# A second v buffer, a single g buffer, ungated output weights and an earlier first weight load in a fused attention and MLP kernel

## The chip, the cores and the metric

The kernel runs on one core of one Trainium2 chip. The metric is the device time of one execution in microseconds (us), lower is better. Before the change the median was 353.1 us (three executions, 352.37 to 354.01). Every number below comes from a timed run or from the trace of a profiled run on the chip. The profiled span is about 2 us shorter than the time of the same execution, so spans are compared with spans and times with times.

## The reference

Causal attention with a forget gate over 8 batches x 8 heads x 576 tokens x 64, and then a two-layer MLP with exact gelu on its 4608 x 512 result:

```python
scores = scale * np.matmul(q, k.transpose(0, 1, 3, 2))
cum = np.cumsum(np.log(np.clip(f, 0.0001, 1.0)), axis=-1)
scores = np.where(causal, -1e9, scores + cum[..., :, None] - cum[..., None, :])
attn = softmax(scores)                       # over the last axis
x = np.matmul(attn, v)                       # heads side by side: 4608 x 512
h = x @ w_in                                 # 512 x 2048
out = gelu(h) @ w_out                        # 2048 x 512
```

## The kernel before

TensorE (PE in the profile) does everything large: scores, attention times v, gemm1 (x times w_in), gemm2 (gelu result times w_out). gemm2 of a batch is spread as filling between the attention steps of the next batch, and then gemm1 of that next batch runs in one stretch, with ScalarE (ACT) taking the gelu of each 128 x 512 result into one of 16 g tiles. GpSimd (POOL) multiplies v by the decay weights ("weighing") and also issues the loads of q, k and of the weights; SyncE (SP) issues the loads of v and the transposing DMAs.

The parts that the change and the argument touch:

```python
g_pool = ctx.enter_context(tc.tile_pool(name="g", bufs=2))   # 16 tags g0..g15
m_psum = ctx.enter_context(tc.tile_pool(name="m_psum", bufs=2, space=PSUM))
...
v_sb = consts.tile([P, H, NBLK, D], FP32)          # one v buffer
nc.gpsimd.memset(v_sb[:, :, 0, 0:1], 0.0)          # gates the load behind it
load_v(0, 0, 4)                                    # SP's queue
load_qk_tokens(0, 6, 8)                            # GpSimd's queue
load_v(0, 4, 8)
...
# in first_attention (batch 0)
weigh_v(0, 0)
load_w_in(0)
load_w_in(1)
weigh_v(0, 1)
load_qk_tokens(1, 0, 4)
weigh_v(0, 2)
weigh_v(0, 3)
load_w_in(2)
load_w_in(3)
nc.gpsimd.memset(v_sb[:, :, 0, 0:1], 0.0)          # v of batch 1 waits for this
load_v(1, 0, 4)
load_v(1, 4, 8)
load_qk_tokens(1, 4, 8)
...
def x_tail_dma(b):                                 # last 64 tokens of a batch
    nc.sync.dma_start_transpose(
        tails[:, :, b * TL : (b + 1) * TL],
        xt_of[b][D:P].rearrange("p i h d -> p (i h d)"))
...
def gemm1(c, ffb):
    ...                                            # 4 matmuls into a m_psum tile
    nc.scalar.activation(g_of[c][ffb], ps, Act.Gelu)
...
# in the loop over batches, behind the attention of batch 0
if b == 0:
    load_w_out(0)
    x_tail_dma(0)
for ffb in range(n_ff):
    gemm1(b, ffb)
    ...
        if ffb == 9:
            weigh_v(1, 0)
            for c in range(1, 4):
                load_w_out(c)
```

The softmax here doesn't subtract the row's maximum and nothing guards it: scores larger than these inputs give would overflow.

## Time and profile before

| | before |
|---|---|
| time, median of three | 353.1 us |
| profiled span | 350.2 us |
| PE busy | 338.7 us (97%) |
| start of gemm1 of batch 0 | 27.83 us |
| first matmul with w_out | 44.72 us |
| start of gemm1 of batch 1 | 70.90 us |
| batch period in the steady part | 36.57 us |

PE is the bound, and only time in which PE stands still, or is made to, moves the result.

From the page of the kernel before, two groups of instructions (line, engine, operation, out<-in, count, busy time, mean of one in ns, idle time just before them and what ended it), and one group of DMA issues, whose last column is the median time from issue to landing in us:

```profile
L392 PE MATMUL ps<-xT,w_in_sb 128*128 128x512 bf16 x512 | 112.6, 379 | 0.7 <-ACT xT L371 0.6
L430 PE MATMUL ps<-w_out_sb,g 128*128 128x512 bf16 (+2 forms) x208 | 44.3, 363 | 0.0
w_out_sb<-in_moe_w_out_dram POOLq DMA_DIRECT2D x4, 512.0 KB, 9.3
```

Neither gemm waits: 0.7 us of idle time before all gemm1 matmuls, 0.0 before gemm2 of the first and the last batch, which are the ones on this line. The weights of gemm2 land 9.3 us after their issue, as the median of four; the first quarter takes 15.6.

### The profile page before, as it was taken

Reading aid. Unit: us, or ns where it says so; the run is one execution under the profiler, and the core shown is the slowest. Engines: PE = TensorE matmul, PEld = TensorE weight load, DVE = VectorE, ACT = ScalarE, POOL = GpSimd, SP = SyncE. Lnnn points to the kernel's source line nnn. Section 1 sums busy time; section 2 is a strip of 40 time slices with the busy share of each in tenths; the row PEclk is TensorE's granted clock in tenths of the full one; section 3 lists DMA queues with packets and bytes.
Section 4 is the critical chain, followed back from the end, with each engine's and each line's share of the span. In section 5 each row is a group of like instructions: output and inputs, shape, how many; then the busy total and the mean of one; then the engine's idle time right before and its main releaser. Section 6 shows DMA issues by size and latency. Waiting matters only on the chain.

```text
span 350.2 us, 7729 instructions
## 1 busy us (share of the span) xinstructions
PE 338.7 (97%) x3082; PEld 174.8 (50%) x3082; DVE 203.0 (58%) x499; ACT 216.1 (62%) x298; POOL 124.5 (36%) x243
## 2 busy tenths in 40 slices
PE   8998989999999999999999999999999999999995
PEld 3564534544555455545554455445544554444443
DVE  4561984496469935894579557956696563011011
ACT  5877585457874687468746874687567774603600
POOL 8291185415538044613453245514350530000000
PEclk9999999999999999999999999999999999999999
DMA  7999989974994998298928794679510131011013
GB/s 108 181 176 196 199 143 195 214 175 95 206 163 136 136 206 156 85 135 137 220 76 128 143 196 99 104 135 213 126 37 2 47 85 45 0 62 60 0 32 90
DMA packets 101219, 43.24 MB, mean 123 GB/s; under 512 B 80000, under 2 KB 96640, under 8 KB 101184
## 3 DMA queue, kind: packets, MB, share of 16 engines
q1 hardware_dynamic: 83888, 28.60, 40.1%
q0 software_dynamic: 16896, 13.63, 26.0%
q8 instruction: 24, 0.39, 0.5%
q10 hardware_dynamic: 400, 0.52, 0.4%
q14 instruction: 11, 0.09, 0.1%
HBM read 36.85 MB, written 9.44 MB: 132 GB/s over the span
## 4 chain that ended last, share of the span: by engine, by line
PE 83%; ACT 9%; POOL 2%; issue 2%; DMA 2%; SPq 1%; DVE 0%; ACTq 0%; POOLq 0%
PE ps L392 36%; PE ps L479 18%; PE ps L430 12%; PE o L332 9%; PE s L296 7%; ACT e L311 5%; ACT L311 2%; DMA v_sb<-in_v_dram 2%; ACT g L404 1%; POOL vw L279 1%; PE ps_x L368 1%; SPq L114 1%; POOL k L102 1%; POOL q L102 0%; PE s L305 0%
## 5 line engine op out<-in xcount | busy, mean ns | idle before, releaser
L404 ACT ACTIVATE g<-ps 128x512 bf16<-128x512 f32 x144 | 86.0, 597 | 82.2 <-PE ps L392 82.2
L311 ACT ACTIVATE e<-s 128x896 bf16<-128x896 f32 (+1 forms) x128 | 103.9, 862 | 30.7 <-PE s L296 25.5
L392 PE MATMUL ps<-xT,w_in_sb 128*128 128x512 bf16 x512 | 112.6, 379 | 0.7 <-ACT xT L371 0.6
L479 PE MATMUL ps<-w_out_sb,g 64*128 64x512 bf16 (+1 forms) x690 | 102.4, 376 | 0.0
L313 POOL TENSOR_SCALAR_AFFINE_SELECT e<-e 128x256 bf16<-128x256 bf16 x135 | 53.4, 406 | 113.5 <-ACT e L311 112.5
L392 PEld LDWEIGHTS <-w_in_sb 128*128 128x128 bf16 x576 | 56.0, 98 | 68.1 <-issue 2.9
L279 POOL TENSOR_TENSOR vw<-v_sb,wT 128x640 bf16<-128x640 f32 x32 | 41.0, 1280 | 47.5 <-DMA v_sb<-in_v_dram 15.8
L296 PE MATMUL s<-qT,kT 64*128 64x320 bf16 (+4 forms) x384 | 47.9, 282 | 4.0 <-ACT e L311 3.4
L479 PEld LDWEIGHTS <-g 64*128 64x128 bf16 (+1 forms) x690 | 37.7, 94 | 25.4 <-issue 1.6
L263 DVE COPY qT<-tq 64x288 bf16<-64x288 bf16 x96 | 45.1, 470 | 1.5
L332 PEld LDWEIGHTS <-e 128*128 128x128 bf16 x960 | 35.9, 98 | 17.6 <-issue 11.5
L430 PE MATMUL ps<-w_out_sb,g 128*128 128x512 bf16 (+2 forms) x208 | 44.3, 363 | 0.0
L332 PE MATMUL o<-vw,e 128*128 128x65 bf16 x960 | 41.7, 194 | 0.8 <-ACT e L311 0.4
L487 DVE COPY ot<-ps 128x512 f32<-128x512 f32 x24 | 16.5, 689 | 36.0 <-PE ps L479 36.0
L439 DVE COPY ot<-ps 128x512 f32<-128x512 f32 (+2 forms) x13 | 8.4, 650 | 48.9 <-PE ps L430 48.7
L296 PEld LDWEIGHTS <-kT 64*128 64x128 bf16 x384 | 20.1, 94 | 28.7 <-issue 15.6
L263 DVE COPY kT<-tk 64x288 bf16<-64x288 bf16 x96 | 32.3, 336 | 1.6
L347 DVE RECIPROCAL r<-o 128x5 f32<-128x5 f32 x64 | 12.5, 195 | 30.1 <-PE o L332 29.3
L348 DVE TENSOR_TENSOR x<-o,r 128x256 bf16<-128x256 f32 x64 | 27.2, 425 | 2.2
L430 PEld LDWEIGHTS <-g 128*128 128x128 bf16 x208 | 18.8, 98 | 18.9 <-issue 0.4
L358 DVE TENSOR_SCALAR xt<-o,r 64x64 bf16<-64x64 f32 x60 | 17.4, 290 | 1.4
L489 DVE TENSOR_TENSOR ot<-ot,ps 128x512 f32<-128x512 f32 x24 | 16.5, 687 | 1.3
(60 smaller groups left out, 144.7 us busy)
## 6 DMA issues: line engine op xcount, KB each, us to landing
out_dram<-ot SPq DMA_DIRECT2D x32, 256.0 KB, 2.4
v_sb<-in_v_dram SPq DMA_DIRECT2D x20, 256.0 KB, 4.6
v_sb<-in_v_dram SPq DMA_DIRECT2D x29, 128.0 KB, 5.5
q<-in_q_dram POOLq DMA_DIRECT2D x6, 576.0 KB, 6.5
k<-in_k_dram POOLq DMA_DIRECT2D x6, 576.0 KB, 8.6
w_in_sb<-in_moe_w_in_dram POOLq DMA_DIRECT2D x4, 512.0 KB, 7.9
w_out_sb<-in_moe_w_out_dram POOLq DMA_DIRECT2D x4, 512.0 KB, 9.3
q<-in_q_dram POOLq DMA_DIRECT2D x4, 144.0 KB, 4.4
```

What stands on the lines that cost most here:

```text
L263: nc.vector.tensor_copy(rows[:, odd], src[odd * D : (odd + 1) * D, 2 * i + h].rearrange("d j p -> d p j"),)
L279: nc.gpsimd.tensor_tensor(vw_of[b][:, hs, :, 0:D], v_sb[:, hs, :, :], w.unsqueeze(3).to_broadcast([P, 2, NBLK, D]), Alu.mult,)
L296: nc.tensor.matmul(st[:, h, c : c + w], kT[i][d, K0[n] : K0[n] + P], qT[i][d, q0 : q0 + w], start=True, stop=not on_pe or c not in SDIAG[t],)
L311: nc.scalar.activation(et[:, :, 0:c], st[:, :, 0:c], Act.Exp, scale=scale)
L313: nc.gpsimd.affine_select(out=et[:, :, c0 : c0 + P], in_=et[:, :, c0 : c0 + P], compare_op=Alu.is_ge, fill=0.0, base=0, pattern=[[0, 2], [ ...
L332: nc.tensor.matmul(o[:, m, :], e_of[b, i, t][:, h, c : c + P], vw_of[b][:, 2 * i + h, n, :], start=(n == 0), stop=(n == m),)
L348: nc.vector.tensor_tensor(x_of[b, i][:, :, h, :], o[:, 0:4, 0:D], r[:, 0:4].unsqueeze(2).to_broadcast([P, NBLK - 1, D]), Alu.mult,)
L358: nc.vector.tensor_scalar(*tail, r[D:P, 4:5], None, Alu.mult)
L392: nc.tensor.matmul(ps, w_in_sb[:, kt, ffb * P : (ffb + 1) * P], src[:, kt, :], start=(kt == 0), stop=(kt == n_dm - 1),)
L404: nc.scalar.activation(g_of[c][ffb], ps, Act.Gelu)
L430: nc.tensor.matmul(pss[ts][:, c0:c1], g_of[c][kt][:, ts * P : (ts + 1) * P], w_out_sb[:, kt, c0:c1], start=(kt == 0), stop=(kt == n_ff - 1),)
L479: nc.tensor.matmul(banks[r], g_of[c][kt][rows, ts * P : (ts + 1) * P], w_out_sb[rows, kt, :], start=(kt == 0), stop=last if r else kt == n ...
```

## The change

The intent: bring the loads of the first 50 us forward. v gets a second buffer, so v of batch 1 is queued right behind v of batch 0 instead of waiting until that one has been weighed. The four w_out quarters are queued without the former gates, behind w_in and q and k of batch 1. The first w_in quarter is issued ahead of the first weighing. And the g tiles go from two buffers to one.

```diff
-    g_pool = ctx.enter_context(tc.tile_pool(name="g", bufs=2))
+    g_pool = ctx.enter_context(tc.tile_pool(name="g", bufs=1))
...
-    v_sb = consts.tile([P, H, NBLK, D], FP32)
+    v_of = [consts.tile([P, H, NBLK, D], FP32, name=f"v_sb{i}") for i in range(2)]
...
     load_v(0, 4, 8)
+    load_v(1, 0, 4)
+    load_v(1, 4, 8)
...
+    nc.vector.memset(v_of[1][0:D, :, 4, :], 0.0)
...
+        gate = x_pool.tile([P, 1], FP32, tag="gate", name="gate")
+        nc.gpsimd.tensor_copy(gate, v_of[0][:, 0, 2, 0:1])
+        load_w_in(0)
         weigh_v(0, 0)
-        load_w_in(0)
         load_w_in(1)
...
-        nc.gpsimd.memset(v_sb[:, :, 0, 0:1], 0.0)
-        load_v(1, 0, 4)
-        load_v(1, 4, 8)
         load_qk_tokens(1, 4, 8)
+        for c in range(4):
+            load_w_out(c)
...
         if b == 0:
-            load_w_out(0)
             x_tail_dma(0)
...
                     weigh_v(1, 0)
-                    for c in range(1, 4):
-                        load_w_out(c)
+                    weigh_v(1, 1)
                     load_qk_tokens(2)
-                    weigh_v(1, 1)
```

More of the change, by code (lines that the diff above doesn't have):

```diff
@@ L114, in load_v @@
             nc.sync.dma_start(
-                v_sb[p0:P, h0:h1, n, :],
+                v_of[b % 2][p0:P, h0:h1, n, :],
                 v[b, h0:h1, K0[n] + p0 : K0[n] + P].rearrange("h p d -> p h d"),
@@ L136 @@
     )
-    nc.gpsimd.memset(v_sb[:, :, 0, 0:1], 0.0)
+    nc.gpsimd.memset(v_of[0][:, :, 0, 0:1], 0.0)
     load_v(0, 0, 4)
@@ L172 @@
     nc.scalar.activation(lf, f_sb, Act.Ln)
-    nc.vector.memset(v_sb[0:D, :, 4, :], 0.0)
+    nc.vector.memset(v_of[0][0:D, :, 4, :], 0.0)
     nc.vector.tensor_tensor_scan(cum, ones, lf, 0.0, Alu.mult, Alu.add)
     nc.scalar.activation(wk, cum, Act.Exp, bias=cum[:, S // 2 : S // 2 + 1], scale=-1.0)
+    nc.vector.memset(v_of[1][0:D, :, 4, :], 0.0)
     def warm_up(n):
@@ L280, in weigh_v @@
             vw_of[b][:, hs, :, 0:D],
-            v_sb[:, hs, :, :],
+            v_of[b % 2][:, hs, :, :],
             w.unsqueeze(3).to_broadcast([P, 2, NBLK, D]),
@@ L541, in first_attention @@
         load_w_in(3)
-        nc.gpsimd.memset(v_sb[:, :, 0, 0:1], 0.0)
-        load_v(1, 0, 4)
-        load_v(1, 4, 8)
         load_qk_tokens(1, 4, 8)
+        for c in range(4):
+            load_w_out(c)
         scores(0, 2, 0)
```

## The prediction

> **What bounds the kernel now.** I began with the page. TensorE (PE) is busy nearly all the time; ScalarE, VectorE and GpSimd are far from it.
>
> ```profile
> PE 338.7 (97%) x3082; PEld 174.8 (50%) x3082; DVE 203.0 (58%) x499; ACT 216.1 (62%) x298; POOL 124.5 (36%) x243
> ```
>
> So PE idles 350.2 - 338.7 = 11.5 us in all, and nothing can gain more than that. The windows view says where: a steady batch (144 to 181 us) has PE busy 36.70 of 37.00 us, the last 58 us idle 3.6 (mostly the closing stores), the first 70 us some 6. The change works on loads of the first 50 us, so I read that part instruction by instruction. In the timeline (start, duration, what, and the idle time before it with what ended it), only one PE gap there is ended by weighted v, which is what the change wants to bring forward:
>
> ```profile
> 15.00 1.28 POOL L279 TENSOR_TENSOR vw<-v_sb,wT 128x640 bf16<-128x640 f32 x1 [6.53 <-DMA v_sb<-in_v_dram]
> 16.36 1.58 POOL L155 DMA_DIRECT2D w_in_sb<-in_moe_w_in_dram  x2
> 17.95 1.30 POOL L279 TENSOR_TENSOR vw<-v_sb,wT 128x640 bf16<-128x640 f32 x1
> 19.46 0.64 PE L332 MATMUL o<-vw,e 128*128 128x65 bf16 x15 [0.28 <-POOL vw L285]
> ...
> 42.79 1.28 POOL L279 TENSOR_TENSOR vw<-v_sb,wT 128x640 bf16<-128x640 f32 x1 [15.65 <-PE ps L392]
> 44.16 2.31 POOL L159 DMA_DIRECT2D w_out_sb<-in_moe_w_out_dram  x3
> ```
>
> GpSimd waits 15.65 us for v of batch 1 (its fourth DMA of the first half was issued at 26.9 and took 15.3 us to land, 42.2), and w_out queues behind that. But in the view of waits PE never waits for w_out, w_in or batch 1's vw. These late loads are hidden.
>
> The diff has one more line: g goes from two buffers to one. So I read ScalarE around the switches between exp (L311) and gelu (L404):
>
> ```profile
> 63.81 0.70 ACT L311 ACTIVATE e<-s 128x640 bf16<-128x640 f32 x1 [0.36 <-PE s L296]
> 64.54 1.28 ACT L404 ACT_TABLE_LOAD   x1
> 71.96 0.60 ACT L404 ACTIVATE g<-ps 128x512 bf16<-128x512 f32 x1 [6.14 <-PE ps L392]
> ...
> 84.91 0.60 ACT L404 ACTIVATE g<-ps 128x512 bf16<-128x512 f32 x1 [0.27 <-PE ps L392]
> 85.52 1.28 ACT L311 ACT_TABLE_LOAD   x1
> ```
>
> The gelu table is loaded at 64.54, right after the last exp, 6 us before the first gemm1 matmul at 70.90. It costs nothing, in all seven later batches alike (the last is at 286.42, first gelu 291.67).
>
> **What the Trainium skill says.** "ScalarE: Activation LUTs", What ACT_TABLE_LOAD costs: a load takes about 1283 ns, plus a drain of about 1380. The trace agrees on the load (1.28 us) but shows no such drain: from load to first exp it is 86.82 - 85.52 = 1.30. "Perfetto Trace Analysis", Identifying Dependency Chains: an instruction that waits for several engines may get event-semaphore instructions put ahead of it. The trace has these, and what they cost is below. "DMA: Bandwidth & Descriptors", Queues, rings and completion order: each DMA engine takes turns between the queues that have work. So v of batch 1, behind v of batch 0 in the same queue, cannot delay it, but takes a share from the weights on GpSimd's queue. The before trace fits: v of batch 1 took up to 15.3 us to land beside the weights, v of batch 0 at most 6.1.
>
> **The change part by part.** I compared the instruction streams of the two builds, which gives order and waits, no times. PE's stream is the same row for row. Four things differ.
>
> 1. Weighing. One w_in issue (0.8 us) instead of two lies between the first two weighings, so the second comes 0.8 us earlier: the 0.28 gap at 19.46 closes. The first weighing keeps its 15.00: the gate waits for the third v DMA (issued 7.7, landed after 5.9, so 13.6), the w_in issue then ends near 14.5, and the fifth v DMA lands at 14.86. Gain 0.28 us.
>
> 2. VectorE clears the second v buffer (0.48 us, as L173) between the scan, which ends at 6.15, and the first kT copy, so that copy starts near 6.65 instead of 6.31 and ends at 7.41. The first scores start at 7.53, behind warm-up matmuls that end at 7.50. Loss at most 0.05 us.
>
> 3. v, w_out and q, k of batch 2 come earlier. PE waited for none of them: gain 0. Could v delay the weights? It is 8 x 576 x 64 x 4 = 1.18 MB. From 15 to 20 us the DMA moved 98 GB/s against some 200 when full, so about 5 x 102 KB = 0.5 MB fits in idle time; the other 0.7 MB pushes what is queued then by at most 3.4 us. Landing times before, plus 3.4, against first use: batch 1's first half of k 28.1, 31.5, used at 34.3; third w_in quarter 31.0, 34.4, used at 35.4. Nothing is late, though the last has only 1 us.
>
> 4. One g buffer. gemm2 of a batch has ended, in PE's order, before gemm1 of the next begins, so the data are free in time. But each gelu now also carries a wait on ScalarE's own semaphore, and with two waits the first is put on the instruction ahead. For the first gelu of batches 1 to 7 that is the table load: in the stream of after these seven loads wait for PE and the gelu behind waits only for ScalarE. Since that gelu needs its PSUM tile, the wait on the load must be the one for gemm1's first group. The load comes onto the path. This is my main term.
>
> Its size, from single records and semaphore updates of the trace (batch 1): first gemm1 matmul 70.896; the fourth's semaphore 71.934. A table load that waits for PE exists already at exp of batch 1: semaphore 44.381, load 44.448 (0.067 later), exp 45.742. So the first gelu starts at 71.934 + 0.067 + 1.294 = 73.295 instead of 71.957 and ends 0.597 later at 73.892. m_psum has two buffers, so gemm1's third group waits for this gelu; a stalled PE resumes 0.05 after it ends (batch 0: 0.04 to 0.05), 73.94, instead of 72.620. Stall 1.32 us, and PE is the bound, so it is all paid: 7 x 1.32 = 9.2 us.
>
> The second wait costs too. A gelu with one wait starts 0.023 us after PE's semaphore; an instruction with two has the event semaphore ahead and starts 0.083 after. In batch 1 PE's third group starts 0.057 after the semaphore of the gelu's end and needs about 0.042: slack 0.015, and 0.06 more makes a stall of 0.045 per pair of groups. The before kernel shows exactly this in its final gemm1, whose gelus have two waits already:
>
> ```profile
> 72.82 0.60 ACT L404 ACTIVATE g<-ps 128x512 bf16<-128x512 f32 x1 [0.27 <-PE ps L392]
> 74.55 0.60 ACT L404 ACTIVATE g<-ps 128x512 bf16<-128x512 f32 x1 [0.27 <-PE ps L392]
> ...
> 320.30 0.60 ACT L404 ACTIVATE g<-ps 128x512 bf16<-128x512 f32 x1 [0.34 <-PE ps L392]
> 322.07 0.60 ACT L404 ACTIVATE g<-ps 128x512 bf16<-128x512 f32 x1 [0.31 <-PE ps L392]
> ```
>
> 1.77 for two groups there, 1.73 in batch 1. After the table stall six pairs remain in a batch: 6 x 0.045 = 0.27, x 7 = 1.9 us. The final gemm1 pays already. The last gelu of a batch is 0.06 later, and the chain from it to the exp table and exp sets when PE goes on:
>
> ```profile
> 84.91 0.32 ACT g L404
> 85.22 0.30 issue
> 85.52 1.19 ACT L311
> 86.71 0.11 issue
> 86.82 0.93 ACT e L311
> 87.74 0.04 issue
> 87.78 0.37 PE s L296 x2
> ```
>
> For six of the seven batches an exp follows: 6 x 0.06 = 0.4 us.
>
> Sum: 9.2 + 1.9 + 0.4 - 0.28 + 0.05 = 11.3 us. 353.1 + 11.3 = 364.4 us.
>
> **The rivals.** (a) As intended: the loads come earlier and time falls. For it: GpSimd waits 15.8 us for v and 15.6 at L279. Against: GpSimd is 36% busy and PE's stream waits for it only 0.28. It would give 352 to 353. (b) The single buffer costs nothing, because the load's wait is met early (if it were gemm2's old reads, done at about 70.8, the load would end near 72.2, and only 0.2 us a batch be lost): 354 to 356. Against: the wait must cover the first group's tile. (c) The load is exposed but the two-wait term is absorbed: 353.1 + 9.0 = 362. Against: the final gemm1 shows it. (d) Weights collide with v and gemm1 of batch 0 stalls at its third quarter: 1 to 2 us on top, 366. For it: the margin of 1 us; against: before, v already competed with that very quarter.
>
> **Range and chances.** (c) and (d) bound the likely outcomes, with 0.8 us for the scatter of the before runs (352.37 to 354.01): 362.2 to 366.2. The line of 2% lies at 360.2, 4 us below my sum; to stay under it the table term would have to halve, and it rests on an exact wait and on a load length that every table load of the trace shows. Slower 0.93, within 2% 0.06, faster 0.01.
>
> **What would show it.** In the profile after: seven gelu table loads with an idle time before them ended by PE ps and the gelu 1.29 later; a PE gap of about 1.3 us in gemm1 before its third group, ended by ACT g; gelus spaced 1.77 per pair in batches 1 to 7; the batch period 36.6 going to about 38.2; no PE gap at the second weighed pair; GpSimd's 15.65 us wait gone without effect. I am wrong if the loads still run right after the last exp, or if PE's gap is elsewhere.

## More of the kernel before

From PE's timeline of the kernel before (start, duration, what, and in brackets the idle time before it with what ended it), the place where the first w_out quarter is needed:

```profile
44.60 0.29 PE L305 MATMUL s<-after,ident_bf 128*128 128x128 bf16 x2
44.72 1.03 PE L430 MATMUL ps<-w_out_sb,g 128*128 128x512 bf16 x4
```

The first w_out matmul follows without a gap at 44.72. By the trace's records this quarter had landed at 41.98, 2.7 us earlier.

## The result and the profile after

The changed kernel took 369.38 us (median of four executions: 367.37, 369.38, 369.38, 370.50), against 353.56 us of the kernel before on the same chip. The ratio is 1.043, with a 95% interval of 1.035 to 1.051: slower. Ratios here are the mean time of the fast executions of one kernel over the mean of those of the other from the same rounds, so they are not quite the ratio of the medians. The predicted 364.4 us had the direction right; the time lies 3 us above the predicted range (362.2 to 366.2).

The page of the changed kernel, in the lines that answer to those of before (its L396, L408 and L434 are L392, L404 and L430 of before):

```profile
PE 342.2 (94%) x3040; PEld 175.5 (48%) x3082; DVE 203.4 (56%) x500; ACT 215.5 (59%) x298; POOL 124.5 (34%) x243
...
L396 PE MATMUL ps<-xT,w_in_sb 128*128 128x512 bf16 x503 | 114.6, 378 | 9.5 <-ACT g L408 8.1
...
L434 PE MATMUL ps<-w_out_sb,g 128*128 128x512 bf16 (+2 forms) x200 | 44.0, 366 | 2.5 <-DMA w_out_sb<-in_moe_w_out_dram 1.9
...
L408 ACT ACT_TABLE_LOAD x8 | 10.3, 1283 | 39.6 <-PE ps L396 39.5
...
w_out_sb<-in_moe_w_out_dram POOLq DMA_DIRECT2D x4, 512.0 KB, 23.0
```

Three things are new. PE idles 365.3 - 342.2 = 23.1 us in place of 11.5. gemm1 waits 8.1 us for gelus, and the gelu table loads now wait for PE: that was predicted. And gemm2's first matmul waits 1.9 us for w_out, whose loads now take 23.0 us from issue to landing in place of 9.3 (medians of four; the first quarter 20.6 in place of 15.6): that was not.

**The predicted part.** ScalarE's timeline of the changed kernel around the switch to gelu in batch 2:

```profile
114.27 1.28 ACT L408 ACT_TABLE_LOAD   x1 [5.53 <-PE ps L396]
115.56 1.08 ACT L408 ACTIVATE g<-ps 128x512 bf16<-128x512 f32 x2
117.33 0.60 ACT L408 ACTIVATE g<-ps 128x512 bf16<-128x512 f32 x1 [0.68 <-PE ps L396]
118.19 0.60 ACT L408 ACTIVATE g<-ps 128x512 bf16<-128x512 f32 x1 [0.27 <-PE ps L396]
119.10 0.60 ACT L408 ACTIVATE g<-ps 128x512 bf16<-128x512 f32 x1 [0.31 <-PE ps L396]
```

The table load waits 5.53 us for PE's first gemm1 group; in the kernel before it ran directly behind the last exp. The gelu starts 1.29 us after it. From there the gelus come 1.77 us a pair (117.33 to 119.10) where before they came 1.73 a pair. PE's timeline, batch 1, shows what this does:

```profile
77.79 6.54 PE L396 MATMUL ps<-xT,w_in_sb 128*128 128x512 bf16 x28 [1.16 <-ACT g L408]
```

**The part that was not predicted.** PE's timeline of the changed kernel where w_out is first needed:

```profile
45.84 0.29 PE L309 MATMUL s<-after,ident_bf 128*128 128x128 bf16 x2
48.05 0.60 PE L434 MATMUL ps<-w_out_sb,g 128*128 128x512 bf16 x1 [1.92 <-DMA w_out_sb<-in_moe_w_out_dram]
...
51.50 1.03 PE L434 MATMUL ps<-w_out_sb,g 128*128 128x512 bf16 x4
```

PE waits 1.92 us, and the first matmul after the wait takes 0.60 us. The clock records say why: PE runs at half clock from 48.09 to 51.50 us. The Trainium skill, "TensorE: Matmul & The Clock Gate", What's actually happening, describes a free-running window of 3413 ns over which TensorE's activity is watched to set the clock; the records agree with the length, 3.413 us.

Why was w_out late? It was issued at 27.38 us, 1 us later than before (26.37), but landed at 48.00 in place of 41.98. The windows view of the changed kernel gives, for each stretch of time, the busy time of each engine with the number of instructions, then the granted clock, the DMA share and the DMA rate in GB/s:

```profile
38.00:41.70 3.70, 3.65 (x21) 1.71 (x20) 3.57 (x8) 2.12 (x4) 0.00 (x0) 1.00 1.25 195
41.70:46.10 4.40, 4.40 (x38) 2.13 (x36) 4.24 (x10) 2.80 (x5) 0.00 (x0) 1.00 1.63 38
46.10:50.00 3.90, 1.76 (x6) 0.53 (x6) 1.74 (x4) 2.60 (x3) 0.00 (x0) 0.75 1.25 203
```

For 4.4 us the DMA engines moved 38 GB/s, while their packets show as in flight all along (a share of 1.63, for packets of two queues at once); before and after that they moved 195 and 203. In the packet records, 26 packets of both queues stand for up to 4.3 us and are all released between 46.07 and 46.13 us, just as the last DMA of v of batch 1 lands (46.15). Directly behind that DMA in SP's queue stands the transposing DMA of the first x tail:

```profile
32.33 5.12 SPq L384 DMA_TRANSPOSE tails<-xt  x1
```

It was issued at 32.33 and landed at 47.93. In the kernel before, it was issued at 42.54, when GpSimd's queue was nearly empty, and landed 2.46 us later.

**The sum of the profiled runs.** The first and the last column of numbers are positions in PE's timeline, in us; the three between them are the lengths of the parts from one position to the next. The second trace of the changed kernel and the two mended kernels are explained under the experiments.

| kernel | gemm1 of batch 0 starts | from there to the first w_out matmul | from there to gemm1 of batch 1 | from there to PE's end | PE's end |
|---|---|---|---|---|---|
| before | 27.83 | 16.89 | 26.18 | 275.54 | 346.44 |
| changed | 29.07 | 18.98 | 26.70 | 286.83 | 361.58 |
| changed, second trace | 29.14 | 20.67 | 26.74 | 286.87 | 363.42 |
| changed, tail moved | 27.80 | 16.89 | 26.17 | 286.85 | 357.71 |
| changed, tail moved, table loaded early | 28.14 | 16.88 | 26.17 | 278.21 | 349.40 |

The first changed row against before: 1.24 + 2.09 + 0.52 + 11.29 = 15.14 us. The last term is the predicted one, 9.2 + 1.9 + 0.4 = 11.5. The second and third are the late w_out and the half clock after it. The first is a late start, in which PE happened to stay at half clock until 10.54 us (before: until 5.24).

### The profile page after: what moved, and what is told of

The parts are those of the page before. It is cut to its first block, busy times and chain, and to the rows that moved or that the text cites. A ratio compares the mean times of both kernels' runs of the same rounds, so it can differ in the third digit from the quotient of the medians.

```text
span 365.3 us, 7799 instructions
## 1 busy us (share of the span) xinstructions
PE 342.2 (94%) x3040; PEld 175.5 (48%) x3082; DVE 203.4 (56%) x500; ACT 215.5 (59%) x298; POOL 124.5 (34%) x243
## 4 chain that ended last, share of the span: by engine, by line
PE 72%; ACT 11%; DMA 6%; issue 4%; POOL 4%; SPq 2%; DVE 0%; ACTq 0%; POOLq 0%
PE ps L396 28%; PE ps L483 17%; PE ps L434 12%; PE o L336 8%; PE s L300 6%; DMA w_out_sb<-in_moe_w_out_dram 6%; ACT e L315 4%; ACT g L408 3%; SPq L114 2%; ACT L315 2%; ACT L408 2%; POOL vw L283 1%; POOL k L102 1%; POOL q L102 1%; PE ps_x L372 1%
## 5 line engine op out<-in xcount | busy, mean ns | idle before, releaser
L396 PE MATMUL ps<-xT,w_in_sb 128*128 128x512 bf16 x503 | 114.6, 378 | 9.5 <-ACT g L408 8.1
L408 ACT ACTIVATE g<-ps 128x512 bf16<-128x512 f32 x144 | 85.2, 597 | 54.9 <-PE ps L396 54.7
L483 PE MATMUL ps<-w_out_sb,g 64*128 64x512 bf16 (+1 forms) x666 | 96.2, 377 | 1.0
L396 PEld LDWEIGHTS <-w_in_sb 128*128 128x128 bf16 x576 | 55.5, 97 | 79.5 <-issue 19.6
L283 POOL TENSOR_TENSOR vw<-v_sb,wT 128x640 bf16<-128x640 f32 x32 | 40.9, 1277 | 27.4 <-PE o L336 11.0
L434 PE MATMUL ps<-w_out_sb,g 128*128 128x512 bf16 (+2 forms) x200 | 44.0, 366 | 2.5 <-DMA w_out_sb<-in_moe_w_out_dram 1.9
L267 DVE COPY qT<-tq 64x288 bf16<-64x288 bf16 x96 | 43.4, 452 | 1.5
L336 PEld LDWEIGHTS <-e 128*128 128x128 bf16 x960 | 35.8, 98 | 17.1 <-issue 10.9
L267 DVE COPY kT<-tk 64x288 bf16<-64x288 bf16 x96 | 34.1, 355 | 1.6
L434 PEld LDWEIGHTS <-g 128*128 128x128 bf16 x208 | 18.9, 98 | 21.4 <-DMA w_out_sb<-in_moe_w_out_dram 2.1
```

The costliest lines, as they stand in the source:

```text
L267: nc.vector.tensor_copy(rows[:, odd], src[odd * D : (odd + 1) * D, 2 * i + h].rearrange("d j p -> d p j"),)
L283: nc.gpsimd.tensor_tensor(vw_of[b][:, hs, :, 0:D], v_of[b % 2][:, hs, :, :], w.unsqueeze(3).to_broadcast([P, 2, NBLK, D]), Alu.mult,)
L336: nc.tensor.matmul(o[:, m, :], e_of[b, i, t][:, h, c : c + P], vw_of[b][:, 2 * i + h, n, :], start=(n == 0), stop=(n == m),)
L396: nc.tensor.matmul(ps, w_in_sb[:, kt, ffb * P : (ffb + 1) * P], src[:, kt, :], start=(kt == 0), stop=(kt == n_dm - 1),)
L434: nc.tensor.matmul(pss[ts][:, c0:c1], g_of[c][kt][:, ts * P : (ts + 1) * P], w_out_sb[:, kt, c0:c1], start=(kt == 0), stop=(kt == n_ff - 1),)
L483: nc.tensor.matmul(banks[r], g_of[c][kt][rows, ts * P : (ts + 1) * P], w_out_sb[rows, kt, :], start=(kt == 0), stop=last if r else kt == n ...
```

## The experiments

An execution is called slow here when it is more than 1.5% above the fastest of the same kernel. Where a kernel itself has two kinds of executions, this rule calls the longer kind slow, and the ratio of the fast runs leaves it out. Where that happens below, all times are listed.

### 1. One g buffer alone (g1_only)

```diff
 # the kernel before
-    g_pool = ctx.enter_context(tc.tile_pool(name="g", bufs=2))
+    g_pool = ctx.enter_context(tc.tile_pool(name="g", bufs=1))
```

> The kernel before with one edit: one g buffer instead of two. Theory (the table load and the second wait come onto the path): +11.3 us, 364 to 365 us, ratio about 1.032; seven gelu table loads that wait for gemm1's first group, a PE gap of about 1.2 us ended by ACT g in each of batches 1 to 7, gelus 1.77 us apart per pair, and no PE wait for w_out. Rival (the loads that come early did the harm, the single g buffer is cheap): 353 to 355 us.

Measured: 363.64 us (362.88 to 364.26) against 352.77, ratio 1.030 (1.028 to 1.033). PE waits 8.1 us in seven waits for the gelu, as in the changed kernel, and never for w_out. So the single g buffer alone costs 10.9 us, two thirds of the loss, and the rest belongs to the loads.

### 2. One g buffer, gelu table loaded early (g1_preload)

```diff
 # the kernel before with g bufs=1, and
+    tab = consts.tile([P, 2], FP32)
+    nc.vector.memset(tab, 0.0)
...
                 scores(b, i, t)
+                if (i, t) == (HP - 1, 3):
+                    nc.scalar.activation(tab[:, 1:2], tab[:, 0:1], Act.Gelu)
...              # and the same two lines in second_attention
```

A gelu of one column behind the last exp of batches 1 to 7 makes the table load run there, where ScalarE has nothing to wait for.

> The kernel before with one g buffer, and a gelu of a 128x1 tile behind the last exp of batches 1 to 7, so that the gelu table is loaded there, without a wait. Theory: the 7 x 1.32 = 9.2 us of the load go, the second wait (1.9 + 0.4 us) and the small gelus stay: 353.5 + 2.3 = 355 to 356 us. Rival 1 (the load was not the cost, the second wait is): 362 to 364 us. Rival 2 (only the load costs): 353 to 354 us.

Measured: 355.52 us (355.05 to 356.79), ratio 1.008 (1.005 to 1.011). Of the 10.9 us, 8.1 are gone, and with them the table's place on the path. ScalarE's timeline of this run (gelu is L406 here):

```profile
65.43 0.20 ACT L638 ACTIVATE tab<-tab 128x1 f32<-128x1 f32 x1
71.62 0.60 ACT L406 ACTIVATE g<-ps 128x512 bf16<-128x512 f32 x1 [5.98 <-PE ps L394]
72.48 0.60 ACT L406 ACTIVATE g<-ps 128x512 bf16<-128x512 f32 x1 [0.27 <-PE ps L394]
73.39 0.60 ACT L406 ACTIVATE g<-ps 128x512 bf16<-128x512 f32 x1 [0.31 <-PE ps L394]
```

What is left is the alternation of 0.27 and 0.31, the 1.77 us a pair: 2.75 us in all, from the second wait of each gelu, with the extra gelu included.

### 3. The changed kernel with two g buffers (after_g2)

```diff
 # the changed kernel
-    g_pool = ctx.enter_context(tc.tile_pool(name="g", bufs=1))
+    g_pool = ctx.enter_context(tc.tile_pool(name="g", bufs=2))
```

> The changed kernel with two g buffers: the loads moved alone. In the profile of the changed kernel PE waited 1.9 us for the first w_out quarter and then ran at half clock for 3.4 us. Theory (the early v of batch 1 takes queue shares from the weights, w_out comes late): PE waits for w_out again, 1 to 4 us over before, 355 to 358 us, table loads hidden. Rival (that wait was a chance stall of the DMA of one execution, packets of 4.3 us, and the late clock at the start was chance too): 353 to 354 us and no PE wait for w_out.

Measured: 352.37, 353.69, 354.54 and 357.88, 358.06, 358.16 us; median 356.21; the ratio of the fast three is 1.000 (0.996 to 1.004). It builds and runs: there was room for the second v buffer and both g buffers. The loads alone gain nothing, and half of the executions are some 4 us longer, at mean clocks of 0.985 to 0.995 (no trace of one of these was kept). The profiled one is of the short kind, and yet its DMA moved 32 GB/s from 41.3 to 45.1 us, w_out landed at 47.63, and PE waited 0.4 us for it. What it lost came mostly earlier: PE ran at half clock from 28.69 to 32.10 us, just as gemm1 of batch 0 began, and the way from there to the first w_out matmul took 18.97 us in place of 16.89. In this run another wait shows:

```profile
23.38 0.63 PE L336 MATMUL o<-vw,e 128*128 128x65 bf16 x15 [1.09 <-POOL vw L289]
```

The weighed v of the third head pair is late, by 1.09 us, since the last DMA of v of batch 0 landed at 21.66 us; in the kernel before it had landed at 17.17.

### 4. The same, with v of batch 1 held back (g2_v1_late)

```diff
 # the changed kernel with two g buffers
-    load_v(1, 0, 4)
-    load_v(1, 4, 8)
...
         load_w_in(3)
+        nc.gpsimd.memset(v_of[1][:, :, 0, 0:1], 0.0)
+        load_v(1, 0, 4)
+        load_v(1, 4, 8)
```

> As after_g2, but v of batch 1 is held back to where it stood in before, behind the third and fourth w_in quarters; two v buffers, early first w_in quarter and ungated w_out stay. Theory (v's share makes w_out late): w_out's first quarter lands near 42 us instead of 48, PE does not wait for it, 353 to 354 us. Rival (w_out waits for another reason: its own queueing, the transposes of the tails, a stall): the same time and wait as after_g2.

Measured: 353.11 to 355.18 us, median 354.05, ratio 1.003 (1.001 to 1.006). The first w_out quarter lands at 41.33 and PE doesn't wait for it. But a stall is still there; it has moved. From 51.5 to 53.8 us the DMA moves 68 GB/s, and it ends as the last DMA of v of batch 1 lands, now at 53.76, with the transposing DMA behind it (issued 44.47, landed 55.90). The stall follows that pair in the queue, not the clock time and not w_out. It no longer meets a need of w_out, but it meets another: GpSimd waits 2.28 us for v of batch 1 to weigh it, its masking of the exp results comes behind that, and PE waits 1.9 us for the masked results at 56.5 and 58.2 us. From the first w_out matmul to gemm1 of batch 1 this trace needs 28.44 us in place of 26.18.

### 5. The tail's transpose moved away (g2_tail_late)

```diff
 # the changed kernel with two g buffers
-        if b == 0:
-            x_tail_dma(0)
...
 # at the end of second_attention
+        x_tail_dma(0)
         x_tail_dma(b)
```

> Edit: the changed kernel with two g buffers, and the DMA transpose of the first x tail moved from behind v of batch 1 to just ahead of the second x tail's. Theory (a DMA transpose queued right behind v of batch 1, while weights flow in the other queue, holds all transfers up until v of batch 1 is in): no stall of about 4 us between 41 and 46 us, the first w_out quarter lands at 44 us or earlier, the PE has no wait for w_out above 0.2 us, and no fast-or-slow split of the runs (358 against 353 us): about 353 us. Rival (v of batch 1 itself, sharing the engines with the weights, makes the stall): the stall of 3 to 4 us stays at the same place, w_out lands at 47 us or later, and the runs split again.

Measured: 351.61 to 353.46 us in five executions and one of 357.39; median 352.66, ratio 0.999 (0.996 to 1.003). No packet of the first 50 us stands longer than 1.5 us, w_out lands at 43.76, PE doesn't wait for it. The one long execution has a match in the kernel before (357.07 us in the same rounds, both at a mean clock of 0.981), so it is not of this kernel.

### 6 and 7. The first w_in quarter put back (g2_w_in_late), and both edits (g2_both_late)

```diff
 # the changed kernel with two g buffers
-        gate = x_pool.tile([P, 1], FP32, tag="gate", name="gate")
-        nc.gpsimd.tensor_copy(gate, v_of[0][:, 0, 2, 0:1])
-        load_w_in(0)
         weigh_v(0, 0)
+        load_w_in(0)
```

> Edit: the changed kernel with two g buffers, and the first weighing put back ahead of the first w_in quarter's issue, which loses its gate. Theory (issuing the first w_in quarter ahead of the weighing makes it share the engines with the second half of v of batch 0): that half lands at 17 to 18 us in place of 21.7 to 22.1, and the PE no longer waits 1.1 us for the weighed v; the w_out stall at 41 to 46 us stays. About 353 to 355 us. Rival (the late v is from v of batch 1 in the same queue, not from w_in): v of batch 0 still lands after 20 us.

> Edit: both edits of the two runs before it. Theory: neither wait, 352.5 to 353.5 us, the same as before within 0.3%, so that nothing but these two side effects and the single g buffer separates the changed kernel from the one before. Rival: still 354 us or more, then a third cause is open.

Measured: 353.79 us (352.94 to 356.93), ratio 1.004 (1.000 to 1.007), and 353.63 us (353.14 to 356.23), ratio 1.003 (1.000 to 1.007). The first half of the expectation holds: all of v of batch 0 has landed by 18.00 and 18.02 us, and PE never waits for weighed v. So the earlier w_in quarter has a part in the delay of v. It is not the whole of it: in experiment 4 that quarter is issued early too, at 14.41 us, but v of batch 1 is held back, and all of v of batch 0 has landed by 18.20. In the seven traces that have both, an early w_in quarter and v of batch 1 queued behind v of batch 0, the last of v of batch 0 lands at 20.76 to 22.10. So it takes both, by one trace without the one and two without the other. The second half fails twice. The stall did not come in the profiled run of g2_w_in_late, though the transpose stands in its old place: the DMA moved 174 GB/s from 39.0 to 42.7 us. (There v of batch 1 was in at 42.76, only 0.4 us after the k ahead of w_out; in the stalled traces of experiments 3 and 8 and of the first run it was still under way, to 45.1 us or later. Whether that decides it was not tested.) And a new wait came in both: now w_in and k of batch 1 are later, and PE waits 0.93 and 1.13 us at 42.4 and 42.8 us for k. Moving one load ahead of another in this stretch only moves the wait, since the DMA engines are full: they move 193 to 195 GB/s from 23 to 38 us in the trace of g2_w_in_late.

### 8. The changed kernel again (after_again)

> The changed kernel again, unedited, for a second trace. Theory: the late w_out quarter is of the kernel and recurs (landing after 46 us, a PE wait of 1 to 3 us, then a half-clock stretch of about 3.4 us), while the half clock up to 10.5 us in the first trace is chance and need not recur (half clock until 5 to 7 us as in the other traces). Time 366 to 370 us. Rival: the half clock at the start is a product of the change and recurs to 10 us.

Measured: 363.20, 369.02, 369.18, 369.94 us. The profiled execution (369.18) shows the stall again, and longer: 27 GB/s from 42.5 to 47.8 us, w_out landing at 49.76, a PE wait of 3.62 us, then half clock from 50.79 to 54.20. The half clock at the start ended at 6.42 us in this trace, so the 10.54 us of the first are not of every run (experiment 10 has 9.82, all other traces 4.66 to 6.61); the start was late nonetheless, with a 1.20 us wait for the k of the second head pair. Of the eight executions of the changed kernel seven took 367 to 371 us at mean clocks of 0.984 to 0.995, and one took 363.20 at a clock of 1.000: the time that the single g buffer alone explains.

### 9 and 10. The changed kernel with only the tail moved (after_tail_late), and with a plain DMA in its place (after_tail_copy)

```diff
 # the changed kernel, g bufs=1 kept; after_tail_late:
-        if b == 0:
-            x_tail_dma(0)
...
+        x_tail_dma(0)          # at the end of second_attention
         x_tail_dma(b)
 # after_tail_copy: this too, where the transpose had been
+        if b == 0:
+            xs = xt_of[0][D:P].rearrange("p i h d -> p (i h d)")
+            nc.sync.dma_start(out=junk[D:P, 0 : xs.shape[1]], in_=xs)
```

> Edit: the changed kernel, one g buffer kept, with only the DMA transpose of the first x tail moved from behind v of batch 1 to just ahead of the second x tail's. Theory (that transpose, queued behind v of batch 1 while the weights flow, makes the stall; the stall makes the late w_out quarter; that makes the 369 us): the 363.2 us that one of eight runs of the changed kernel reached becomes the rule, 363 to 364 us in nearly all runs, no stall above 2 us between 40 and 50 us, no PE wait for w_out above 0.2 us. Rival (v of batch 1 and the weights alone make it): 367 to 370 us in most runs, as in the changed kernel.

> Edit: as the run before it, and in the place that the transpose left, an ordinary DMA of the same source into an unused tile. Theory (it is the transposing DMA that stalls the others): no stall, 363 to 364 us in nearly all runs. Rival (any DMA that hangs there in the queue does it): a stall of 3 to 5 us ends as v of batch 1 lands, and 367 to 370 us in most runs.

Measured: 363.35 us (362.89 to 364.93) and 364.04 us (363.21 to 364.71), six executions each, not one at 367 or above. The ratios are 1.030 (1.026 to 1.035) and 1.032 (1.027 to 1.036), within the interval of the single g buffer alone. The same window as in the stall, first with the tail moved:

```profile
41.70:46.10 4.40, 3.96 (x27) 1.64 (x26) 4.25 (x9) 3.05 (x5) 0.00 (x0) 1.00 1.24 204
```

and with the plain DMA in the transpose's place:

```profile
41.70:46.10 4.40, 4.40 (x39) 2.22 (x38) 4.24 (x10) 2.80 (x5) 0.00 (x0) 1.00 1.24 207
```

204 and 207 GB/s in place of 38. The plain DMA stood in the same place of the queue (issued at 33.32 us, landed at 47.74, behind v of batch 1 at 47.07) and held nothing up: w_out landed at 44.37. So it is the transposing DMA, queued behind a load while the other queue is full, that stalls both queues. That settles what parts 363 from 367 to 370 us. (These runs were on another chip than experiment 8; but the kernel before takes 352.4 us there and 352.6 on the chip of experiments 5 and 8, where moving the transpose removed the stall as well.)

### 11. Both repairs, with one g buffer (after_mended)

The edit is that of after_tail_late and that of g1_preload in the changed kernel.

> Edit: the changed kernel, one g buffer kept, with the transpose of the first x tail moved as in the two runs before it, and with a gelu of one column behind the last exp of batches 1 to 7, which loads the gelu table early. Theory (the table load is 8 us, the stalled w_out quarter 5 to 6 us, the second wait 2 to 3 us, and these add): 355 to 356 us. Rival (they overlap, or something else is in the 16 us): 358 us or more.

Measured: 355.54 us (354.84 to 356.10), ratio 1.008 (1.004 to 1.012). The causes add: 369.1 to 369.4 (the two medians of the changed kernel) with all three, 363.35 without the stall, 355.54 without the table load too, and 352.66 with the second g buffer (experiment 5). In the last row of the table above, the part behind gemm1 of batch 1 is 278.21 - 275.54 = 2.67 us longer than before, which is the second wait of the gelus, with the seven small gelus included.

### 12. Three g buffers in the kernel before (before_g3)

```diff
 # the kernel before
-    g_pool = ctx.enter_context(tc.tile_pool(name="g", bufs=2))
+    g_pool = ctx.enter_context(tc.tile_pool(name="g", bufs=3))
```

> Edit: the kernel before with three g buffers in place of two. Theory (with two buffers, only the gelus of the last batch but one meet a buffer that is not yet free, and wait for two things): they take 1.73 us a pair in place of 1.77, so at most 0.3 us in all: 352.3 to 352.8 us, the same. Rival (the g buffers of the kernel before cost something in every batch): faster by 1 us or more.

Measured: 352.60 us (351.53 to 356.94), ratio 0.999 (0.995 to 1.004): the same. In its trace the gelus of the last gemm1 come every 0.86 us with gaps of 0.27, so 1.73 a pair where before there were 1.77, and each of them starts 0.023 us after PE's semaphore where before it was 0.083. This confirms that the second wait comes from the g tile; the gain of about 0.3 us that the expectation allows is too small for this interval to show.

No version beat the kernel before. The two best, g2_tail_late and before_g3, are equal to it within their intervals. That fits the first line of the prediction: PE idled 11.5 us in all, and hardly any of it waited for these loads.

## Why the prediction was right and wrong

**The main term of step 4, the table load: right.** Predicted 7 x 1.32 = 9.2 us. The traces show seven loads that wait for PE, the gelu 1.29 us later, and a PE gap of 1.16 us in the waits view, where ends are modelled. By starts alone, which are measured, the third group of gemm1 begins 3.05 us after the first matmul in all seven batches of the changed kernel, and 1.72 to 1.73 before (1.82 in one batch): 1.32 us each, as predicted. Loading the table early gave back 8.1 us (experiment 2) and 7.8 us (363.35 - 355.54, experiment 11). The repaired kernel's seven batches each keep one more pair of slow gelus, 7 x 0.045 = 0.3 us by the prediction's own figure, and run one more small gelu; what else is missing to 9.2, under 1 us, was not traced.

**The second wait: right in kind, a little low.** Predicted 1.9 + 0.4 = 2.3 us, measured 2.67 to 2.75 in the mended kernels, which hold 0.3 us more of it for the reason just given. The batch period became 38.20 us, as predicted. The whole of step 4 came out at 11.29 us from gemm1 of batch 1 to the end, against 11.5.

**Step 1, the weighing: no gain, and at times a loss.** It said the gap of 0.28 us at 19.46 closes and that v of batch 1 "behind v of batch 0 in the same queue, cannot delay it". The gap did close. The sentence on the queue, an inference and not what the skill's page says, doesn't hold: with v of batch 1 held back, v of batch 0 was in by 18.20 us, with it behind by 21.66 (experiments 4 and 3). And the other mover was left out: the first w_in quarter, issued at 14.49 in place of 16.36, shares the DMA engines with the second half of v of batch 0. The last two DMAs of that half landed at 20.82 and 21.55 in place of 16.98 and 17.17 us. GpSimd shows it in its timeline of the changed kernel:

```profile
19.58 0.67 POOL L102 DMA_DIRECT2D k<-in_k_dram  x1
21.76 1.28 POOL L283 TENSOR_TENSOR vw<-v_sb,wT 128x640 bf16<-128x640 f32 x1 [1.50 <-DMA v_sb<-in_v_dram]
```

PE paid nothing in that trace, since it was late already, and 1.09 us in experiment 3. The step asked whether the first weighing stays at its time (it came at 15.30 in place of 15.00) and did not ask about the third. Experiments 4 and 6 together show the cause. The 15.65 us wait, too, was read too simply: the profile puts its end down to PE, at 42.79, and v had landed 0.55 us earlier. It was gone in the changed kernel without effect, as the prediction said.

**Step 2, VectorE's memset: not seen.** No PE wait for it appears in the traces; the first kT copy starts at 6.57 us in place of 6.31, much as predicted. At 0.05 us its cost could not be separated from the start of gemm1, which varies from 27.4 to 29.1 us over the traces of all kernels.

**Step 3, "Nothing is late, though the last has only 1 us": this is the step that failed.** It went through k and the third w_in quarter and left out the first w_out quarter. Its own rule, the landing before plus 3.4, gives 41.98 + 3.4 = 45.4 us against a first use at 44.72: late by 0.7 us. That would have named the wait, but for the wrong reason. In the four traces with all early loads and no stall (experiments 5, 9, 10 and 11) the quarter landed at 43.76 to 44.37 us, and PE did not wait for it. What was wrong is the bound itself: that v of batch 1 pushes the weights back "by at most 3.4 us" takes a full DMA rate of some 200 GB/s as given. In fact the rate fell to 38 GB/s for 4.4 us, and w_out landed 6.0 us later than before. No trace of before could show that, because there the transpose ran when GpSimd's queue was empty. But what would stand beside what was there to be read in the comparison of the two builds: the transpose stays right behind v of batch 1 in SP's queue, and the four w_out quarters now flow in the other queue at the same time.

The cost of that step: w_out landing 6 us later, a PE wait of 1.92 us (3.62 in the second trace) and then 3.41 us at half clock, of which 0.5 us remained as net loss at the start of gemm1 of batch 1. In the timed runs it is 369.1 to 369.4 less 363.35, some 6 us. The two traces account for 2.6 us (2.09 + 0.52) and 4.3 us (3.78 + 0.56) by the stall and its half clock; another 1.3 us in each is the late start, which comes before the stall and is not its work. The runs without a trace have mean clocks down to 0.984. By an estimate from the 0.995 of the traced runs, which have one half-clock stretch each, that is about three stretches; where they lay is not known. Without the stall the changed kernel takes 363.35 us, inside the predicted range.

**The rivals.** Rival (d), "Weights collide with v and gemm1 of batch 0 stalls at its third quarter", named the right kind of trouble in the wrong place: gemm1 of batch 0 never stalled on w_in. Rivals (a), (b) and (c) are out: the loads alone gain nothing (experiment 5), and both terms of the single buffer are measured.

**What stays open.** How a transposing DMA holds up both queues is not shown by these records, only that it does and when. It didn't in the profiled run of experiment 6, where the last w_out quarter was issued at 31.85 us in place of 29.58, and not in one of eight executions of the changed kernel, if that one's time and clock are read in this way; what decides it was not found. Part of the late start of the two changed traces (1.24 and 1.31 us) goes with the clock and with the landing of one k, and neither comes in every trace. Whether the change has a share in it was not tested, but the traces hint at one: gemm1 of batch 0 starts at 27.43 to 27.83 us in the four traces with the loads of before, and at 27.80 to 29.14 in the ten with the changed loads.

## What to carry to other kernels

Before halving a buffer to make room for another, see what each writer of the buffer waits for now, and on which instruction that wait lands: here a second wait pushed the first onto a table load and turned a free 1.28 us into 1.3 us on the path of each batch. The room was not even needed, since both buffers fitted. When loads move earlier, write down landing and first use of every load that shares the engines, the unchanged ones too, and read for each moment what now stands beside what in the other queues; a transposing DMA between loads deserves a question of its own. And where the bound engine waits for none of the loads, moving them can only lose.

## What the Trainium skill lacked or had wrong

- "DMA: Bandwidth & Descriptors", Rules for kernel authors, says that a transpose next to ordinary DMAs "needs nothing". That is so for correctness: all results here were right. It says nothing of time. A transposing DMA queued behind loads in SP's queue, with GpSimd's queue full, took both queues from 195 to 38 GB/s for 4.4 us (27 GB/s for 5.3 us in a second run), and an ordinary DMA in its place left 207.
- "ScalarE: Activation LUTs", What ACT_TABLE_LOAD costs, adds a drain of about 1380 ns to the load. In every trace of this case, where the activation behind a load has nothing else to wait for, it follows 1.29 to 1.30 us after the start of a load of 1.28 us, so no drain shows.
- No page that was looked up gives the price of a second wait on an instruction. Here the instruction starts 83 ns after the semaphore in place of 23, and where the slack was 15 ns this cost 2.7 us over seven batches. Nor does one say that the first of two waits can land on the table load ahead of the activation.
- "TensorE: Matmul & The Clock Gate", What's actually happening, has the window of 3413 ns right (records of 3.413 us), but gives at least one idle window of about that length as what brings the half clock back. Here a wait of 1.92 us was followed by a half-clock window at once. Worked out from the clock records and PE's busy times (modelled at their ends) of all 14 traces: every change of the clock falls on a multiple of 3.413 us from the first one of its trace. Of the windows so cut, from the first full clock to PE's last matmul, three were followed by half clock, and PE was idle in them for 1.61 (experiment 3, no single wait above 0.61), 1.92 and 2.5 us; in all the others it was idle for at most 1.44 us.
